# A two-branch spectral filter on one core: strided PSUM writes in the d transform, weights in 128-partition transfers, and a fold moved to VectorE

## The chip, the cores and the metric

The kernel runs on one core of a Trainium2 chip. The metric is the device time of one execution, in microseconds (us), as the median of several runs. Engines are named as in the profile: PE is TensorE's matrix multiply, PEld its weight load, DVE is VectorE, ACT is ScalarE, POOL is GpSimd, SP is SyncE, which here only issues transfers. An "eviction" is the copy of a PSUM tile to SBUF as bf16 by ACT or DVE.

## What is computed

Two filters A and B work on the same input `x` (2048 rows, 1024 columns, bf16). Each takes the real two-dimensional Fourier transform of `x`, multiplies it with its own complex weights (2048 x 513) and transforms back. A gate per row mixes the two.

```
x = A_x
g = _sigmoid((x * gate_w).sum(-1, keepdims=True))
X = rfft2(x)                                   # the same for both filters
a = irfft2(X * (A_w_r + 1j * A_w_i)).astype(bfloat16)
b = irfft2(X * (B_w_r + 1j * B_w_i)).astype(bfloat16)
return g * a + (1 - g) * b
```

## The kernel before, in words

The 2048 rows are 128 x 16, and the transform along the rows is split accordingly, so the whole work is a chain of matmuls with constant matrices. Its stages, with the names that the code gives them:

- **x fold** (`fS`, `fT`, lines 593 to 602). For each of eight pairs of row groups, DVE adds and subtracts the halves of the columns (two instructions of 128x1024).
- **S1** (line 604, 16 of them). Eight matmuls of 256 columns each: the second fold of the columns is done by accumulation, with F and its negative side by side as the moving operand. The eviction is called `Z`. All sixteen `Z` must be there before the next stage starts.
- **Gate** (`gate_row`, `zg`), small matmuls on `Z`.
- **D** (line 637, 16 of them, kg = 0 to 15): the transform along the columns (d), eight matmuls of 256 columns into one PSUM tile of 1024 columns. Four groups of 256 columns stand side by side, and the eviction `Q` (line 651) interleaves two and two of them, so it writes SBUF with a stride of two elements.
- **S2** (line 654, 16 of them): the second part of the row transform, on `Q`; eviction `X`. X is now the spectrum.
- **Products** (`prod`, line 676; eight for each filter, called PA and PB here): DVE multiplies two kg's of X with the weights, two `mul` of 128x2048 and two `sum` of 128x1024.
- **I1** (line 692, 16 for each filter), first part of the inverse; eviction `V`. The column 512 goes a way of its own in small pieces (`x512`, `p512`, `v512`: p5, v5, v5t), and a small transfer (`vrow`) puts it into `V`.
- **Dinv** (line 752, 16 for each filter); eviction `VA` for filter A and `VB` for B.
- **S1i** (line 809, 16): mixes A and B through gate matrices (`gmix` makes them: sig, RA, RB) and does the last row transform; eviction `o`. DVE then unfolds the columns (`h0`, `h1`, `y0`, `y1`), and a transfer takes each pair of row groups out.

The weights are loaded in three chunks of kg (4, 4 and 8; `KC`, line 16), each chunk in two halves of 64 partitions (`pm`), real and imaginary apart (`wpart`, line 515): fourteen transfers a filter, as the first chunk's second half takes two. In the first half of the partitions a chunk is one contiguous run for each partition, in the second half the rows run backwards, each row of 513 elements (1026 bytes) by itself. B's weights go into the memory that held F, so they wait until S1 is over.

**What sets the order.** A planner (`Plan.run`, line 287) is part of the kernel's program. It gives each operation an assumed cost and a rank (`ORDER`, line 18: a start and a step for each kind of work), plays the engines through, and each engine's instructions are emitted in the order that comes out; an eviction goes to ACT or DVE, whichever is free first in that play. On the chip each engine then works its list strictly in that order, with semaphore waits where data comes from another engine. [...] Lines 454, 457, 479, 480 and 485 are the helpers that record all matmuls, all DVE arithmetic, ACT's evictions, DVE's evictions and all transfers, so the profile's groups are told apart by tiles: `PS<-DM,R` is D, `PS<-RING,SK` S2, `PS<-SK,RING` I1, `PS<-DI,R` Dinv, `PS<-R,RING` S1, `PS<-R,FM` and `PS<-RING,DM` S1i, `PS<-RM,ZG` gmix.

Of the kernel before, what the change touches and what calls it, by code (L numbers as in the profile page):

```python
# [9 lines left out]
ALU = mybir.AluOpType  # L10
# [2 lines left out]

NS = 513
NW = 16 * NS
KC = ((0, 4), (4, 8), (8, 16))
CELL = 512
ORDER = {"in": (0, 0), "x": (48.5, 5.31), "gate": (128.3, 6.12), "D": (35.3, 4.27), "S2": (2.5, 7.29),
         "PA": (46.6, 2.74), "IA": (49.9, 4.36), "x5": (67.7, 12), "row": (123.1, 12), "EA": (124.8, 11.5),
         "PB": (99.2, 5.5), "IB": (130, 4.9), "gm": (54.4, 5.49), "EB": (126.2, 10.71), "S": (130, 12),  # L20
         "U": (0.5, 2.73)}
DEPTH = ((0, 2), (2, 4), (4, 8), (8, 12), (12, 16))


# [6 lines left out]
def make_consts():  # L31
# [45 lines left out]
    for z in range(2):  # L77
        for pm in range(2):
            for k2 in range(16):
                for j in range(4):  # L80
                    po = pm * 64 + k2 * 4 + j
                    i, cj, spec = (3 - j if pm else j), pm == 1, False
                    if z == 1:
                        i, cj = ((0, 1, 0, 1), (2, 3, 3, 2))[pm][j], 32 * j + 16 * pm > 64
                        spec = i == 0
                    for q2 in range(16):
                        w = np.exp(-1j * pi2 * q2 * (k2 + cj) / 16)
                        if spec and j == 2:
# [24 lines left out]
        S2[z, 2] = -S2[z, 1]  # L113
# [144 lines left out]
class Plan:  # L258
# [28 lines left out]
    def run(self, keys):  # L287
# [8 lines left out]
        for n in nodes:  # L296
            for p in n.pre:
                p.suc.append(n)
            for t in n.tiles:
                t.left += 1  # L300
        free = {e: 0.0 for e in Sched.ENG}
        cells = {a: [True] * c for a, c in self.arena.items()}
        used = {}
        ready = {e: [] for e in Sched.ENG}
# [42 lines left out]
        for n in nodes:  # L347
            if not n.wait:
                push(n)
        now, count, done = 0.0, 0, 0  # L350
        while done < len(nodes):
            for e in ("sp", "pool", "pe", "act", "dve"):
                if free[e] > now + 1e-9:
                    continue
                for item in ready[e]:
                    n = item[2]
                    if not take(n):
                        continue
                    occ, lat = n.engs[e]
                    n.eng, n.start = e, now  # L360
                    free[e] = now + occ
                    n.end = now + lat
                    if n.dma:
                        dma_free = max(dma_free, now + 1.3) + lat
                        n.end = dma_free + 0.9
                    order.append(n)
                    count += 1
                    heappush(events, (n.end, count, n))
                    heappush(events, (free[e], -count, None))
                    for e2 in n.engs:  # L370
                        ready[e2].remove(item)
                    break
# [32 lines left out]
def bass_gated_mix__spectral_gfnet__spectral_gfnet__prompt_kernel(  # L405
# [11 lines left out]
    def ap(t, off, dims, p0=0, np_=128):  # L417
# [23 lines left out]
    GW = R4  # L441

    P = Plan({"ps": 8, "ring": NCELL, "late": 32},
             {"ps": ("ps", 4), "p1": ("ps", 8), "st": ("ring", 4), "q": ("ring", 3), "t": ("ring", 2),
              "pp": ("ring", 2), "g": ("ring", 1), "vb": ("ring", 4), "o": ("late", 3), "h": ("late", 2),
              "y": ("late", 3), "w": ("ring", 1)})
    xv = A_x[0].rearrange("(p r) d -> p r d", r=16)
# [43 lines left out]
    def rg(t, off, dims, p0=0, np_=128):  # L491
        return ap(R4 if P.limit[t.pool][0] == "late" else RING, t.at * CELL + off, dims, p0, np_)

    def cload(eng, t, off, key, a, b, keys, **kw):
        dma("c_" + key, eng, lambda: [(ap(t, off, [[1, b - a]]).bitcast(dt.uint16), cst[key].ap()[:, a:b])],
            (b - a) * 256e-6, 400, [], keys, **kw)
# [15 lines left out]
    cload("sp", DM, 0, "DM", 0, 2048, ["DM"])  # L512
    cload("sp", SK, 0, "SK", 0, 1792, ["SK"])

    def wpart(b, ci, pm, c):
        P.key = ("in", 1)
        T = WR[b]
        pt = pit[id(T)]
        k0, k1 = KC[ci]
        src = wsrc[b][c]  # L520
        n = src.shape[-1]
        prs = []

        def part(ka, kb, r0, step):
            o = [[n, kb - ka], [1, n]] if step < 0 else [[1, (kb - ka) * n]]
            i = [[step * n, kb - ka], [1, n]] if step < 0 else [[1, (kb - ka) * n]]
            prs.append((AP(T, 64 * pm * pt + c * NW + ka * NS, [[pt, 64]] + o),
                        AP(src.tensor, src.offset + r0 * n, [[32 * n, 64]] + i)))
        if pm == 0:
            part(k0, k1, k0, 1)  # L530
        else:
            if k0 == 0:
                part(0, 1, 16, 1)
            part(max(k0, 1), k1, 32 - max(k0, 1), -1)
        dma("W%d%d" % (b, ci), "sp", lambda: prs, (k1 - k0) * 0.0657, 205, [], [("W", b, ci, pm, c)],
            after=["F", "FN", "FN1"] if b else [], n=len(prs))

    def wkeys(b, cs=(0, 1, 2)):
        return [("W", b, ci, pm, c) for ci in cs for pm in range(2) for c in range(2)]

    for ci in range(3):
        for pm in range(2):
            for c in range(2):
                wpart(0, ci, pm, c)
    cload("sp", DI, 0, "DI", 0, 2048, ["DI"])
    cload("sp", RM, 0, "RM", 0, 2048, ["RM"])

# [45 lines left out]
    def xrows(n2):  # L593
# [4 lines left out]
        xs = [("x", n2), ("x", n2 + 1)]  # L598
        P.add("fS", vt(1024), lambda e: [tt(rg(st, 0, [[1024, 2], [256, 2], [1, 256]]), lo, hi, ALU.add)], xs, [(st, 0, 1), (st, 2, 3)], alloc=[st])
        P.add("fT", vt(1024), lambda e: [tt(rg(st, 512, [[1024, 2], [256, 2], [1, 256]]), lo, hi, ALU.subtract)], xs, [(st, 1, 2), (st, 3, 4)])  # L600
        for r in range(2):
            stage_s1(n2 + r, st, r)

    def stage_s1(m, st, r):
        P.key = ("x", m)
        t = Tile("p1", 2)

        def fns():
            f = []
            for s in range(2):  # L610
                for h in range(2):
                    o = psl(t, (s * 2 + h) * 256, [[128, 2], [1, 128]])
# [4 lines left out]
        pe("S1", [256] * 8, fns, [(st, 2 * r, 2 * r + 1), (st, 2 * r + 1, 2 * r + 2), "F", "FN" if m < 2 else "FN1"], [(t,)], alloc=[t])  # L617
# [10 lines left out]
    for ci in range(3):  # L628
        for pm in range(2):
            for c in range(2):  # L630
                wpart(1, ci, pm, c)

    allz = [("Z", m) for m in range(16)]
    Q, X = {}, {}
# [2 lines left out]
    def stage_d(kg):  # L637
# [3 lines left out]

        def fns():
            f = []
            for g, o in ((0, 0), (3, 256), (2, 512), (1, 768)):
                for h in range(2):
                    qq = (g in (1, 2)) * 4 + h * 2 + (g & 1)
                    f.append(mm(psl(t, o, [[1, 256]]), ap(R3, qq * 2048 + kg * 128, [[1, 128]]),
                                ap(DM, (2 * g + h) * 256, [[1, 256]]), h == 0, h == 1))
            return f
        pe("D", [256] * 8, fns, allz + ["DM"], [(t,)], alloc=[t])  # L650
        ev("Q", 1024, lambda: (rg(q, 0, [[512, 2], [1, 2], [2, 256]]), psl(t, 0, [[512, 2], [256, 2], [1, 256]])),
           [(t,)], [(q, 0, 2)], slow=True, alloc=[q])

    def stage_s2(kg):
        P.key = ("S2", kg)
# [20 lines left out]
    def prod(b, m):  # L676
# [2 lines left out]
        x = ap(R4, 2 * m * 1024, [[1024, 2], [512, 2], [1, 512]])  # L679
        w = ap(T, 2 * m * NS, [[NS, 2], [NW, 2], [1, 512]])  # L680
        ws = ap(T, 2 * m * NS + NW, [[NS, 2], [-NW, 2], [1, 512]])
        r = [("X", 2 * m), ("X", 2 * m + 1)] + wkeys(b, [0 if m < 2 else 1 if m < 4 else 2])
        p = PT[b, m] = Tile("pp", 4)
        for c, (a, op) in enumerate(((w, ALU.subtract), (ws, ALU.add))):
            t = Tile("t", 4)
# [197 lines left out]
```

## Time and profile before

| | us |
|---|---|
| three runs | 138.89, 141.08, 140.5 (median 140.5) |
| the profiled execution, whole | 138.86 |
| its span, first to last instruction | 137.1 |
| ACT busy | 112.7 in 123 instructions |
| transfers | 19.53 MB |

The difference between the profiled execution and its span, 1.8 us, lies around the instructions. The profiled execution is near the lowest of the three runs. "Busy" of PE counts a matmul from start to modelled end; matmuls overlap, so what a matmul costs in a stream is the distance between two starts, and that is worked out from rows that merge a stream of them.

### The profile page before, as it was taken

To read this page: it belongs to the slowest core of one execution; us is meant where nothing else is said; L and a number is where in the kernel's file an instruction comes from. 1 tells how busy PE (TensorE), PEld (TensorE's weight loads), DVE (VectorE), ACT (ScalarE), POOL (GpSimd) and SP (SyncE) were. 2 spreads that over 40 slices of the span, in tenths; PEclk is the share of its full clock that TensorE was granted. 3 is DMA by queue.
4 is the path that set the end of the run, shared out by engine and by line. 5 is a ranking of instruction groups with operands and counts; after the bars stand their busy time and mean duration, and the time that the engine had idled before them with its cause. 6 is when DMAs were issued, how large, how long until landed. Compare 5 with 4: busy or idle time off the path is not lost.

```text
span 137.1 us, 2504 instructions
## 1 busy us (share of the span) xinstructions
PE 124.1 (91%) x1034; PEld 91.2 (67%) x1034; DVE 118.8 (87%) x159; ACT 112.7 (82%) x123; POOL 0.2 (0%) x4
## 2 busy tenths in 40 slices
PE   6859999999999949999977999999999999999930
PEld 2348886767778627766745888778887757666500
DVE  0399977389999679999999999999996889998992
ACT  6458886879989976999888799999787689898960
POOL 0000000000000000000000000000000000000000
PEclk9999999999999999999999999999999999999997
DMA  4999999999999999992000000000000021465254
GB/s 128 412 428 426 367 197 196 205 213 169 168 341 201 199 194 225 177 164 42 0 0 0 6 0 0 0 5 0 0 1 5 0 108 45 170 244 203 82 226 153
DMA packets 8269, 19.53 MB, mean 143 GB/s; under 512 B 961, under 2 KB 5057, under 8 KB 7618
## 3 DMA queue, kind: packets, MB, share of 16 engines
q1 hardware_dynamic: 8112, 19.36, 54.4%
q8 instruction: 8, 0.13, 0.5%
q10 hardware_dynamic: 146, 0.02, 0.1%
q14 instruction: 3, 0.02, 0.1%
HBM read 15.17 MB, written 4.19 MB: 141 GB/s over the span
## 4 chain that ended last, share of the span: by engine, by line
PE 53%; DMA 16%; DVE 15%; ACT 7%; SPq 3%; issue 3%; DVEq 0%
PE PS L454 53%; DMA R<-in_B_w_i_dram 13%; DVE RING L457 10%; ACT R L479 6%; DMA R<-in_A_x_dram 4%; SPq L485 3%; DVE R L480 3%; DVE R L457 1%; ACT RING L479 1%; DVE RING L480 1%; DVE P L457 0%; ACT V L479 0%; DVEq L215 0%; DVE X L480 0%
## 5 line engine op out<-in xcount | busy, mean ns | idle before, releaser
L479 ACT ACTIVATE R<-PS 128x1024 bf16<-128x1024 f32 x77 | 74.6, 1062 | 10.8 <-PE PS L454 10.6
L457 DVE TENSOR_TENSOR RING<-R 128x2048 bf16<-128x2048 bf16 (+1 forms) x48 | 48.3, 1046 | 6.8 <-DMA R<-in_A_x_dram 4.7
L479 ACT ACTIVATE RING<-PS 128x1024 bf16<-128x1024 f32 x28 | 32.4, 1180 | 4.0 <-PE PS L454 3.7
L454 PE MATMUL PS<-SK,RING 128*128 128x256 bf16 x256 | 31.0, 273 | 2.5 <-DVE R L480 1.9
L454 PE MATMUL PS<-DI,R 128*128 128x256 bf16 x256 | 30.5, 273 | 0.0
L454 PEld LDWEIGHTS PS<-SK,RING 128*128 128x128 bf16 x256 | 23.7, 98 | 7.5 <-DVE R L480 2.2
L454 PEld LDWEIGHTS PS<-DI,R 128*128 128x128 bf16 x256 | 24.7, 98 | 5.3 <-ACT R L479 0.2
L480 DVE CAST R<-PS 128x1024 bf16<-128x1024 f32 x19 | 23.2, 1223 | 4.4 <-PE PS L454 4.3
L457 DVE TENSOR_TENSOR R<-R 128x1024 bf16<-128x1024 bf16 (+1 forms) x36 | 21.3, 629 | 0.5
L457 DVE TENSOR_TENSOR RING<-RING 128x1024 bf16<-128x1024 bf16 x32 | 21.0, 689 | 0.1
L454 PE MATMUL PS<-RING,SK 128*128 128x511 bf16 (+1 forms) x96 | 16.9, 308 | 0.1
L454 PE MATMUL PS<-R,RING 128*128 128x256 bf16 x128 | 14.5, 273 | 2.0 <-DVE RING L457 1.4
L454 PE MATMUL PS<-DM,R 128*128 128x256 bf16 x128 | 16.1, 272 | 0.0
L454 PEld LDWEIGHTS PS<-R,RING 128*128 128x128 bf16 x128 | 12.3, 98 | 4.6 <-DVE RING L457 1.7
L454 PEld LDWEIGHTS PS<-DM,R 128*128 128x128 bf16 x128 | 11.6, 97 | 2.8 <-DVE R L480 0.4
L454 PEld LDWEIGHTS PS<-RING,SK 128*128 128x128 bf16 x96 | 7.7, 97 | 6.8 <-DVE RING L480 0.3
L454 PE MATMUL PS<-R,FM 128*128 128x512 bf16 x32 | 9.5, 379 | 0.4 <-ACT R L479 0.4
L454 PE MATMUL PS<-RING,DM 128*128 128x512 bf16 x32 | 9.5, 379 | 0.0
L480 DVE CAST RING<-PS 128x1024 bf16<-128x1024 f32 x4 | 5.1, 1264 | 3.0 <-PE PS L454 3.0
L454 PEld LDWEIGHTS PS<-RING,DM 128*128 128x128 bf16 x32 | 3.1, 98 | 3.8
L454 PE MATMUL PS<-RING 128*128 128x512 bf16 x10 | 4.4, 631 | 1.2 <-DVE RING L555 1.2
L454 PEld LDWEIGHTS PS<-R,FM 128*128 128x128 bf16 x32 | 3.0, 98 | 2.3 <-ACT R L479 0.9
(33 smaller groups left out, 27.3 us busy)
## 6 DMA issues: line engine op xcount, KB each, us to landing
out_dram<-R SPq DMA_DIRECT2D x7, 512.0 KB, 2.6
R<-in_A_x_dram SPq DMA_DIRECT2D x3, 1024.0 KB, 9.5
R<-in_A_w_r_dram SPq DMA_DIRECT2D x2, 513.0 KB, 19.0
R<-in_A_w_i_dram SPq DMA_DIRECT2D x2, 513.0 KB, 20.8
R<-in_B_w_r_dram SPq DMA_DIRECT2D x2, 513.0 KB, 18.5
R<-in_B_w_i_dram SPq DMA_DIRECT2D x2, 513.0 KB, 20.2
R<-in_A_x_dram SPq DMA_DIRECT2D x2, 512.0 KB, 4.6
R<-in_A_w_r_dram SPq DMA_DIRECT2D x3, 256.5 KB, 15.9
```

What stands on the lines that cost most here:

```text
L454: return lambda e: e.matmul(o, l, r, start=start, stop=stop, skip_group_check=True)
L457: return lambda e: e.tensor_tensor(out=o, in0=a, in1=b, op=op)
L479: return [lambda e: e.activation(o, i, ACT.Copy)]
L480: return [lambda e: e.tensor_copy(o, i)]
L485: lambda e: [lambda q, d=d, s=s: q.dma_start(d, s) for d, s in pairs()],
```

## The change

Four things are changed, and the planner's ranks with them.

1. **D writes PSUM with a stride of two columns.** Two groups of 256 columns are written into the even and odd columns of one 512-column half, so the PSUM tile already has the order that S2 reads. The eviction `Q` becomes a plain copy of 1024 contiguous elements, and the planner no longer counts it as slow.
2. **Weights in 128-partition transfers.** The place of a row in the partitions changes from `pm * 64 + ...` to `2 * (...) + pm` in the constants, so that one kg of one part (real or imaginary) is one transfer over 128 partitions, each partition one row of 1026 bytes: 32 transfers a filter instead of 14. A product waits for the four transfers of its own two kg's, no longer for a chunk.
3. **The last pair's second fold on VectorE.** For the pair of row groups 14 and 15 (`FULL`), DVE does the second fold too (`u0`, `u1`, two instructions of 128x1024), and the two S1 of that pair become eight matmuls of 128 columns each, without accumulation.
4. **A new order.** New ranks in `ORDER`; the planner starts each engine's play at 0.8 to 1.0 instead of 0. The order of PE stays near to the one before; the share of evictions between ACT and DVE shifts.

```
-ORDER = {"in": (0, 0), "x": (48.5, 5.31), "gate": (128.3, 6.12), "D": (35.3, 4.27), "S2": (2.5, 7.29),
-         "PA": (46.6, 2.74), "IA": (49.9, 4.36), "x5": (67.7, 12), "row": (123.1, 12), "EA": (124.8, 11.5),
-         "PB": (99.2, 5.5), "IB": (130, 4.9), "gm": (54.4, 5.49), "EB": (126.2, 10.71), "S": (130, 12),
-         "U": (0.5, 2.73)}
+ORDER = {"in": (0, 0), "x": (78.5, 2.44), "gate": (130, 8.58), "D": (48.2, 3.52), "S2": (38, 2.18),
+         "PA": (74, 0.52), "IA": (58.6, 3.71), "x5": (63.6, 12), "row": (130, 5.98), "EA": (113.2, 12),
+         "PB": (105.1, 3.43), "IB": (129.9, 3.29), "gm": (96.8, 2.63), "EB": (40, 12), "S": (80.6, 8.68),
+         "U": (15.2, 7.24)}
+FULL = (14,)
...
-                    po = pm * 64 + k2 * 4 + j
+                    po = 2 * (k2 * 4 + j) + pm
...
-        free = {e: 0.0 for e in Sched.ENG}
+        free = {"pe": 0.8, "act": 1.0, "dve": 0.8, "pool": 0.8, "sp": 0.9}
...
-    def wpart(b, ci, pm, c):
...
+    def wpart(b, kg, c):
         P.key = ("in", 1)
+        T, src = WR[b], wsrc[b][c]
+        pt, n = pit[id(T)], src.shape[-1]
+        step = 32 - 2 * kg if kg else 16
+        dma("W%d" % b, "sp", lambda: [(AP(T, c * NW + kg * NS, [[pt, 128], [1, n]]),
+                                       AP(src.tensor, src.offset + kg * n, [[32 * n, 64], [step * n, 2], [1, n]]))],
+            0.1313, 300, [], [("W", b, kg, c)], after=["F", "FN", "FN1"] if b else [])
...
+        if n2 not in FULL:
+            for r in range(2):
+                stage_s1(n2 + r, st, r)
+            return
+        u = Tile("u", 4)
+        a, b = (rg2(st, o, [[1024, 2], [512, 2], [1, 256]]) for o in (0, 256))
+        sk, uk = [(st, i, i + 1) for i in range(4)], [(u, 0, 4)]
+        P.add("u0", vt(1024), lambda e: [tt(rg(u, 0, [[1024, 2], [512, 2], [1, 256]]), a(), b(), ALU.add)], sk, [(u, 0, 2)])
+        P.add("u1", vt(1024), lambda e: [tt(rg(u, 256, [[1024, 2], [512, 2], [1, 256]]), a(), b(), ALU.subtract)], sk, [(u, 2, 4)])
         for r in range(2):
-            stage_s1(n2 + r, st, r)
+            stage_s1(n2 + r, u, r, True)
...
+            if full:
+                return [mm(psl(t, ((s * 2 + h) * 2 + i) * 128, [[1, 128]]), rg(st, r * 1024 + s * 512 + i * 256 + h * 128, [[1, 128]]),
+                           ap(R2, m * 128, [[1, 128]]), True, True) for s in range(2) for h in range(2) for i in range(2)]
...
-            for g, o in ((0, 0), (3, 256), (2, 512), (1, 768)):
+            for g, o in ((0, 0), (3, 1), (2, 512), (1, 513)):
...
-                    f.append(mm(psl(t, o, [[1, 256]]), ap(R3, qq * 2048 + kg * 128, [[1, 128]]),
+                    f.append(mm(psl(t, o, [[2, 256]]), ap(R3, qq * 2048 + kg * 128, [[1, 128]]),
                                 ap(DM, (2 * g + h) * 256, [[1, 256]]), h == 0, h == 1))
...
-        ev("Q", 1024, lambda: (rg(q, 0, [[512, 2], [1, 2], [2, 256]]), psl(t, 0, [[512, 2], [256, 2], [1, 256]])),
-           [(t,)], [(q, 0, 2)], slow=True, alloc=[q])
+        ev("Q", 1024, lambda: (rg(q, 0, [[1, 1024]]), psl(t, 0, [[1, 1024]])), [(t,)], [(q, 0, 2)], alloc=[q])
...
-        r = [("X", 2 * m), ("X", 2 * m + 1)] + wkeys(b, [0 if m < 2 else 1 if m < 4 else 2])
+        r = [("X", 2 * m), ("X", 2 * m + 1)] + wkeys(b, (2 * m, 2 * m + 1))
```

More of the change, by code (lines that the diff above doesn't have):

```diff
@@ L15 @@
 NW = 16 * NS
-KC = ((0, 4), (4, 8), (8, 16))
 CELL = 512
-ORDER = {"in": (0, 0), "x": (48.5, 5.31), "gate": (128.3, 6.12), "D": (35.3, 4.27), "S2": (2.5, 7.29),
-         "PA": (46.6, 2.74), "IA": (49.9, 4.36), "x5": (67.7, 12), "row": (123.1, 12), "EA": (124.8, 11.5),
-         "PB": (99.2, 5.5), "IB": (130, 4.9), "gm": (54.4, 5.49), "EB": (126.2, 10.71), "S": (130, 12),
-         "U": (0.5, 2.73)}
+ORDER = {"in": (0, 0), "x": (78.5, 2.44), "gate": (130, 8.58), "D": (48.2, 3.52), "S2": (38, 2.18),
[3 more added lines that the diff above has]
+FULL = (14,)
 DEPTH = ((0, 2), (2, 4), (4, 8), (8, 12), (12, 16))
@@ L349, in run @@
                 push(n)
+        for i, (e, t) in enumerate(free.items()):
+            heappush(events, (t, -1 - i, None))
         now, count, done = 0.0, 0, 0
@@ L368, in run @@
                     heappush(events, (n.end, count, n))
-                    heappush(events, (free[e], -count, None))
+                    heappush(events, (free[e], -9 - count, None))
                     for e2 in n.engs:
@@ L443, in bass_gated_mix__spectral_gfnet__spectral_gfnet__prompt_kernel @@
     P = Plan({"ps": 8, "ring": NCELL, "late": 32},
-             {"ps": ("ps", 4), "p1": ("ps", 8), "st": ("ring", 4), "q": ("ring", 3), "t": ("ring", 2),
+             {"ps": ("ps", 4), "p1": ("ps", 8), "st": ("ring", 4), "u": ("ring", 2), "q": ("ring", 3), "t": ("ring", 2),
               "pp": ("ring", 2), "g": ("ring", 1), "vb": ("ring", 4), "o": ("late", 3), "h": ("late", 2),
@@ L492, in rg, with rg2 @@
         return ap(R4 if P.limit[t.pool][0] == "late" else RING, t.at * CELL + off, dims, p0, np_)
+    def rg2(t, off, dims):
+        return lambda: rg(t, off, dims)
     def cload(eng, t, off, key, a, b, keys, **kw):
@@ L513, in bass_gated_mix__spectral_gfnet__spectral_gfnet__prompt_kernel, with wkeys @@
     cload("sp", SK, 0, "SK", 0, 1792, ["SK"])
-    def wpart(b, ci, pm, c):
+    def wpart(b, kg, c):
         P.key = ("in", 1)
[L517 to L544, printed above, removed]
+        T, src = WR[b], wsrc[b][c]
[4 more added lines that the diff above has]
+            0.1313, 300, [], [("W", b, kg, c)], after=["F", "FN", "FN1"] if b else [])
+    def wkeys(b, kgs=range(16)):
+        return [("W", b, kg, c) for kg in kgs for c in range(2)]
+    for kg in range(16):
+        for c in range(2):
+            wpart(0, kg, c)
     cload("sp", DI, 0, "DI", 0, 2048, ["DI"])
@@ L600, in xrows, with stage_s1 @@
         P.add("fT", vt(1024), lambda e: [tt(rg(st, 512, [[1024, 2], [256, 2], [1, 256]]), lo, hi, ALU.subtract)], xs, [(st, 1, 2), (st, 3, 4)])
+        if n2 not in FULL:
[7 more added lines that the diff above has]
+        P.add("u1", vt(1024), lambda e: [tt(rg(u, 256, [[1024, 2], [512, 2], [1, 256]]), a(), b(), ALU.subtract)], sk, [(u, 2, 4)])
         for r in range(2):
-            stage_s1(n2 + r, st, r)
-    def stage_s1(m, st, r):
+            stage_s1(n2 + r, u, r, True)
+    def stage_s1(m, st, r, full=False):
         P.key = ("x", m)
@@ L616, in fns @@
             return f
-        pe("S1", [256] * 8, fns, [(st, 2 * r, 2 * r + 1), (st, 2 * r + 1, 2 * r + 2), "F", "FN" if m < 2 else "FN1"], [(t,)], alloc=[t])
+        if full:
+            pe("S1", [128] * 8, fns, [(st, 0, 2), (st, 2, 4), "F"], [(t,)])
+        else:
+            pe("S1", [256] * 8, fns, [(st, 2 * r, 2 * r + 1), (st, 2 * r + 1, 2 * r + 2), "F", "FN" if m < 2 else "FN1"], [(t,)])
         ev("Z", 1024, lambda: (ap(R3, m * 8, [[128, 128], [1, 8]]), psl(t, 0, [[8, 128], [1, 8]])), [(t,)], [("Z", m)])
@@ L626, in bass_gated_mix__spectral_gfnet__spectral_gfnet__prompt_kernel @@
           [(gzps,), "MS"], ["ZG"])
[L628 to L631, printed above, removed]
+    for kg in range(16):
+        for c in range(2):
+            wpart(1, kg, c)
     allz = [("Z", m) for m in range(16)]
```

## The prediction

> **What bounds the kernel.** First the page's shares and the chain that ended last, then the waits, then the timeline around the longest wait.
>
> ```profile
> PE 124.1 (91%) x1034; PEld 91.2 (67%) x1034; DVE 118.8 (87%) x159; ACT 112.7 (82%) x123; POOL 0.2 (0%) x4
> ...
> PE 53%; DMA 16%; DVE 15%; ACT 7%; SPq 3%; issue 3%; DVEq 0%
> ```
>
> PE is the busiest engine and half the chain. Its real price shows where a stream is merged:
>
> ```profile
> 94.97 1.06 PE L454 MATMUL PS<-RM,ZG 128*128 128x128 bf16 x16
> ...
> 97.67 7.15 PE L454 MATMUL PS<-DI,R 128*128 128x256 bf16 x64
> ```
>
> 64 matmuls of 256 columns take 7.15 us, the last one 0.27 to drain: 0.109 each, 0.87 for a tile of eight. Those of 128 columns cost (1.06 - 0.22) / 15 = 0.056. A tile of S2 or S1i costs 0.9 (S2 alternates with D in 1.79). So PE has 103 us of work between D's start at 23.71 and its end at 131.3; the rest is waits (view of the waits, 48 to 76 us):
>
> ```profile
> DVE RING L457 <- DMA R<-in_B_w_i_dram: 2.0, 1, 2.0
> PE PS L454 <- DVE R L480: 1.9, 1, 1.9
> ...
> PE PS L454 <- ACT V L479: 1.1, 2, 1.0
> ...
> PE PS L454 <- DVE RING L457: 0.6, 1, 0.6
> ```
>
> The timeline says what the first two are:
>
> ```profile
> 45.46 1.29 DVE L457 TENSOR_TENSOR RING<-RING 128x1024 bf16<-128x1024 bf16 x2
> 48.74 1.23 DVE L457 TENSOR_TENSOR RING<-R 128x2048 bf16<-128x2048 bf16 x1 [1.98 <-DMA R<-in_B_w_i_dram]
> 49.88 1.22 DVE L480 CAST R<-PS 128x1024 bf16<-128x1024 f32 x1
> ...
> 51.16 1.05 PE L454 MATMUL PS<-SK,RING 128*128 128x256 bf16 x8 [1.89 <-DVE R L480]
> ```
>
> DVE stands at B's first product until B's first weights land; behind it waits an eviction, and PE waits for that. PE also waits 0.4 on ACT at 130 us. DVE is second: from its first product (30.49) to its last (95.2) it is full: 16 products at 3.48 (rows 2.36 and 1.29, overlapping), 55.7; five evictions spaced 1.14, 5.7; small pieces 1.3; the weight wait 2.0; together 64.7.
>
> **Part 1, D's strided write.** 128 matmuls change. No row shows a long matmul with a stride in its output. Nearest on PE: I1's weights are read with a stride of two and their LDWEIGHTS takes 98 ns, as D's contiguous ones take 97; S2's 511-column matmul writes from an odd column and takes 378 ns against 380. Farther: ACT writes SBUF with a stride of two in 1.32 instead of 1.02, 29% more. Upper end: 256 columns spread over 512 cost like the 512-column rows (two in 0.43, 0.215 each), 0.107 more each, 13.7 in all. Lower end: 0, for a gain has nothing to come from, since the columns streamed stay 256. I take 0, the PE rows being nearest.
>
> The plain `Q` takes 1.02 on ACT (before 1.33, view by form, 24 to 48 us):
>
> ```profile
> L479 ACT ACTIVATE RING<-PS 128x1024 bf16<-128x1024 f32 x9 | 11.8, 1333 | 1.8 <-PE PS L454 1.8
> L479 ACT ACTIVATE R<-PS 128x1024 bf16<-128x1024 f32 x11 | 10.7, 1049 | 0.4 <-PE PS L454 0.4
> ```
>
> I cost that at 0: PE runs without a wait from 23.7 to 48.2, so ACT's 4 us lie beside it. Without that cover it would be worth two weight-load waits of 0.3 on evicted Q's, 0.6 at most.
>
> **Part 2, the weights.** The trace's packet records give the cause of the late landing: a 4104-byte packet took 160 ns while 128-partition transfers ran beside it, and 316 once only 64-partition ones did. The 1026-byte packets took 102 (median), the fastest 45 to 50. Now 4096 packets a filter on 16 engines: at 51 each (half of 102, as the long ones doubled) 13.1 us; bounds 11.5 (45) and 26.1 (102). SK lands at 17.4, so A lands by 30.5, DI and RM by 33.8, B by 47 instead of 64.6. SP: a weight issue took 0.56 to 0.65 and 0.04 to the next, so 64 need 43 us from 4.7; B's first four go out at about 28 to 31 and land near 33, long before DVE wants them at 46.8. SP's B issues wait for S1 (over by 21.5). Behind them on SP are vrow (wanted near 72) and the outputs, clear of it; POOL issues nothing. More waits stand before DVE's products (four transfers each, not four a chunk): the product at 39.72 had four and started on time, so 0; at most 20 x 0.05 (DVEq's step after the B wait) = 1.0.
>
> So PE's 1.9 goes. What is late next? After: D starts at 22.95 (part 3). DVE's new list puts Q1, Q3, Q4 ahead of the first product: D's fifth tile is done 6.2 later, plus the eviction: 30.4, no earlier than before. Up to PB7 it then holds 16 products (55.7), four evictions (4.6) and small pieces (1.1): the end is 91.8 instead of 95.2. PE reaches the tile that needs it at 95.91 - 0.8 - 3.6 (waits) + 1.0 (below) + 0.87 (one Dinv more ahead) = 93.4, so PE stays the bound. In between, PB1 is done at 30.4 + 9 x 3.48 + 4.6 + 1.1 + 3.48 = 70.9, where PE is at about 70.5; and A's third, sixth and eighth product come within 0.5 of PE's need. I put 1.0 for these four. The 0.6 and the 1.1 of before go, since PA7 (67.3) and the small pieces no longer stand behind the 2.0; ACT's 0.4 goes because the last Dinv of A is moved ahead.
>
> **Part 3, the second fold.** Sixteen S1 matmuls go from 0.109 to 0.056: -0.85. DVE's `u0`, `u1` cost 2 x 0.61 (spacing of the folds): its last fold ends at 18.4, so they end at 19.7, before S1 of row group 14 starts at 20.5: hidden. Z12 behind them is wanted at 19.8. The last Z ends near 22.7 and the three gate tiles (about 1.4) at 22.9: D starts at 22.95, -0.8.
>
> [...]
>
> **Part 4, the order.** PE's list is almost the old one. The tail shifts: from B's first Dinv on DVE has seven evictions where it had four. 28 unfold steps at 0.61, eight short ones at 0.4, seven evictions at 1.14: 28.3 beside PE's 32 tiles, 27.7. DVE has no slack left there, and its last `y` trails PE's end by about 1.0 more than now: +0.9. Bounds: 0 (ACT's share falls by three) and +3.4 (all three evictions exposed).
>
> **Sum**, against the profiled execution (138.86, span 137.07): -0.8 (S1), -4.0 (waits 1.9, 1.1, 0.6, 0.4), +1.0 (new near ties), +0.9 (tail) = -2.9, so 136.0. The median stands 1.64 above that execution. Some of that spread may be the weights' landing, which now is hidden, so I put 0.6 of it on top: 136.6. Alone, this case runs from 134.2 (no near ties, no tail) to 139.0 (tail and DVE's waits exposed).
>
> **Rivals.**
>
> *D's write is slow, and the kernel is slower.* If each written column costs PSUM as much as the pair of columns it lies in, D costs 0.215 a matmul. All 16 D tiles lie before the last S2 on PE, which has no slack there, so +13.7; the near tie at A's sixth product and part of PB1's go, -0.6: 149.7. It decides from 0.025 more a matmul on (3.2 us undo the gain). For it: nothing in the trace excludes it, since no such write is there. Against it: strided reads and odd-start writes on PE cost nothing. With ACT's 29% it would be 0.031 x 128 = 4.0: 140.6, no change.
> [...]
>
> *The weights come no faster.* At 102 ns B's last transfer lands at 17.4 + 2 x 26.1 + 3.3 = 73, B's first four at 50. DVE's `p512` of filter B waits for all of B and now stands near 63, ahead of PA7: DVE loses 2.7 + 6, PE about 7: 143.6. It decides from about 85 ns a packet. Against it: the halving of the 4104-byte packets.
>
> *The waits only move.* DVE is as full as PE: if the near ties cost 1.0 each and the tail its 3.4, -2.9 becomes +2.6: 142 at most, likelier 139.5.
>
> **Chances.** Forecast 0.58; D at twice the price 0.24; D at a part of it 0.08; weights no faster 0.04; waits only move 0.06. The range leaves out the worst of the slow D and the best of the forecast: 134.0 to 150.0; the forecast's own is 134.2 to 139.0. A difference under 2% (137.7 to 143.3 around 140.5) can't be told from no change here. Faster: 0.44, three quarters of the forecast. Within: 0.29, its last quarter, the partly slow D and most of the moved waits. Slower: 0.27, D at twice the price and most of the weights' rival.
>
> **What would show it.** D's group at 272 ns a matmul and its stream at 0.109 says part 1 is free; a step near 0.215 there is the rival. No wait of DVE on in_B_w; B landing near 47. S1 ending 0.8 earlier. PE's waits between 48 and 76 near 1 us. DVE without gaps after 105 us. Wrong would be: a longer D stream, DVE standing at `p512`, or PE waiting for DVE beyond 2 us.

## The result and the profile after

The changed kernel takes 151.28 us (median of four runs, 150.11 to 151.53), the kernel before in the same comparison 139.69 (138.47 to 141.08): ratio 1.0845, 95% interval 1.0719 to 1.0971. It is slower, and its time is close to the 149.7 of the first rival, which had D's write at twice the price. The profiled execution took 151.53, its span is 149.74 (before 138.86 and 137.07).

The page of after, busy shares and the chain that ended last:

```profile
PE 136.2 (91%) x1034; PEld 96.6 (64%) x1034; DVE 119.1 (80%) x160; ACT 110.1 (74%) x124; POOL 0.2 (0%) x4
...
PE 66%; DVE 17%; DMA 7%; issue 5%; ACT 1%; SPq 1%; DVEq 1%
```

PE's share stayed at 91% of a longer span: it has 12 us more work in as many instructions. DVE and ACT have about as much work as before, in a span 12.7 longer. Groups by form, after (mean ns of one behind the busy time, then the idle time before them and what ended it):

```profile
L456 PE MATMUL PS<-DM,R 128*128 128x256 bf16 x128 | 29.6, 417 | 0.0
...
L481 ACT ACTIVATE RING<-PS 128x1024 bf16<-128x1024 f32 x25 | 25.6, 1028 | 13.7 <-PE PS L456 13.7
...
L482 DVE CAST RING<-PS 128x1024 bf16<-128x1024 f32 x7 | 8.6, 1225 | 12.5 <-PE PS L456 12.5
```

D's matmul takes 417 ns where it took 272, as the same group of the kernel before shows:

```profile
L454 PE MATMUL PS<-DM,R 128*128 128x256 bf16 x128 | 16.1, 272 | 0.0
```

The plain eviction `Q` is as short as hoped (1.03 in ACT's row, which holds other evictions too; its twelve `Q` alone take 1.02), and ACT and DVE spend the gain, and more, waiting for PE. PE's timeline where D begins, in after and then before:

```profile
22.64 5.36 PE L456 MATMUL PS<-DM,R 128*128 128x256 bf16 x24
27.79 1.10 PE L456 MATMUL PS<-RING,SK 128*128 128x512 bf16 x6
28.75 1.89 PE L456 MATMUL PS<-DM,R 128*128 128x256 bf16 x8
```

```profile
23.71 2.79 PE L454 MATMUL PS<-DM,R 128*128 128x256 bf16 x24
```

Twenty-four D matmuls in 5.36, the last one 0.417 long: (5.36 - 0.417) / 23 = 0.215 from start to start, where it was (2.79 - 0.272) / 23 = 0.109. A tile of D takes 1.72 instead of 0.87, a tile of S2 beside it 0.96 instead of 0.92.

### The profile page after: what moved, and what is told of

Same layout as the page of the kernel before. It is cut to its first block, busy times and chain, and to the rows that moved or that the text cites. A ratio compares the mean times of both kernels' runs of the same rounds, so it can differ in the third digit from the quotient of the medians.

```text
span 149.7 us, 2569 instructions
## 1 busy us (share of the span) xinstructions
PE 136.2 (91%) x1034; PEld 96.6 (64%) x1034; DVE 119.1 (80%) x160; ACT 110.1 (74%) x124; POOL 0.2 (0%) x4
## 4 chain that ended last, share of the span: by engine, by line
PE 66%; DVE 17%; DMA 7%; issue 5%; ACT 1%; SPq 1%; DVEq 1%
PE PS L456 66%; DVE R L459 9%; DVE RING L459 6%; DMA R<-in_A_x_dram 3%; DMA out_dram<-R 3%; ACT R L481 1%; DVE R L482 1%; DVE RING L482 1%; SPq L487 1%; DVEq L215 1%; DVE P L459 1%
## 5 line engine op out<-in xcount | busy, mean ns | idle before, releaser
L481 ACT ACTIVATE R<-PS 128x1024 bf16<-128x1024 f32 x81 | 78.9, 1053 | 15.7 <-PE PS L456 15.7
L481 ACT ACTIVATE RING<-PS 128x1024 bf16<-128x1024 f32 x25 | 25.6, 1028 | 13.7 <-PE PS L456 13.7
L456 PE MATMUL PS<-DM,R 128*128 128x256 bf16 x128 | 29.6, 417 | 0.0
L459 DVE TENSOR_TENSOR RING<-RING 128x1024 bf16<-128x1024 bf16 x34 | 22.0, 687 | 0.9 <-PE PS L456 0.8
L482 DVE CAST R<-PS 128x1024 bf16<-128x1024 f32 x15 | 18.3, 1223 | 5.2 <-PE PS L456 4.9
L456 PEld LDWEIGHTS PS<-DM,R 128*128 128x128 bf16 x128 | 16.2, 131 | 9.3 <-ACT R L481 0.4
L482 DVE CAST RING<-PS 128x1024 bf16<-128x1024 f32 x7 | 8.6, 1225 | 12.5 <-PE PS L456 12.5
L456 PE MATMUL PS<-R,RING 128*128 128x256 bf16 (+1 forms) x128 | 13.6, 266 | 2.0 <-DVE RING L459 1.4
L456 PEld LDWEIGHTS PS<-RING,SK 128*128 128x128 bf16 x96 | 9.0, 105 | 7.2
L541 ACT ACTIVATE R<-R 128x256 bf16<-128x256 bf16 (+1 forms) x2 | 2.0, 1048 | 3.3 <-DMA R<-c_F 3.3
```

What stands on the lines that cost most here:

```text
L456: return lambda e: e.matmul(o, l, r, start=start, stop=stop, skip_group_check=True)
L459: return lambda e: e.tensor_tensor(out=o, in0=a, in1=b, op=op)
L481: return [lambda e: e.activation(o, i, ACT.Copy)]
L482: return [lambda e: e.tensor_copy(o, i)]
L541: lambda e, a=a, b=b: [lambda e: e.activation(ap(R2, 2048 + a, [[1, b - a]]), ap(R2, a, [[1, b - a]]), ACT.Copy, scale=-1.0)],
```

## The experiments

In the order in which they are told. e1, e3, e4, e5, e7 and e10 to e14 start from the changed kernel, e2, e6, e8 and e9 from the kernel before. "D to last y" runs from D's first matmul to the end of DVE's last unfold, "tail" from the start of PE's last matmul to that end; all are read off the timelines of the profiled executions, one for each kernel.

| kernel | ratio to before (95%) | span | S1 start to D | D to last y | tail |
|---|---|---|---|---|---|
| before | | 137.07 | 17.47 | 110.87 | 3.49 |
| after | 1.0845 (1.0719 to 1.0971) | 149.74 | 16.64 | 124.59 | 4.67 |
| e1 | 0.9927 (0.9879 to 0.9975) | 136.9 | 16.64 | 111.26 | 4.91 |
| e2 | 1.0763 (1.0667 to 1.0859) | 148.8 | 17.97 | 121.82 | 3.49 |
| e5 | 0.9857 (0.9772 to 0.9942) | 135.4 | 16.62 | 109.64 | 4.41 |
| e6 | 0.9850 (0.9817 to 0.9883) | 135.0 | 17.51 | 108.79 | 3.49 |
| e7 | 0.9776 (0.9734 to 0.9818) | 134.5 | 16.62 | 109.10 | 5.01 |
| e8 | 1.0005 (0.9964 to 1.0045) | 137.3 | 17.43 | 111.10 | 3.48 |
| e9 | 0.9686 (0.9562 to 0.9810) | 134.4 | 16.61 | 108.71 | 3.48 |
| e10 | 0.9660 (0.9571 to 0.9749) | 134.7 | 17.08 | 108.50 | 3.84 |
| e12 | 0.9705 (0.9624 to 0.9787) | 133.4 | 16.62 | 108.08 | 3.99 |

By the intervals, after and e2 are more than 2% slower than the kernel before, and e12 is more than 2% faster. So is e10, but the runs of the kernel before beside e9 and e10 scatter most (139.61 to 141.67), so these two ratios are the least sure. e1, e6 and e8 lie within 2% of the kernel before; whether e5, e7 and e9 do can't be told.

**e1: part 1 undone, e2: part 1 alone.** The edit of e1, and of e2 the other way round in the kernel before:

```
-            for g, o in ((0, 0), (3, 1), (2, 512), (1, 513)):
+            for g, o in ((0, 0), (3, 256), (2, 512), (1, 768)):
-                    f.append(mm(psl(t, o, [[2, 256]]), ...
+                    f.append(mm(psl(t, o, [[1, 256]]), ...
-        ev("Q", 1024, lambda: (rg(q, 0, [[1, 1024]]), psl(t, 0, [[1, 1024]])), ...
+        ev("Q", 1024, lambda: (rg(q, 0, [[512, 2], [1, 2], [2, 256]]), psl(t, 0, [[512, 2], [256, 2], [1, 256]])), ...
```

> The changed kernel with part 1 undone: D writes contiguous columns and the eviction Q interleaves them again; weights, fold and the order of every engine stay as in the changed kernel. Theory (D's strided write is the whole loss): D's stream falls from 0.215 to 0.109 a matmul, 13.6 us of PE work go, and the time is 136 to 138.5, that is the prediction's sum for the other three parts. Rival (the rest of the change loses as well, by its order or its 64 transfers): D's stream is as short, but the time stays above 140.

> The kernel before with part 1 alone: D writes with a stride of two, Q is a plain copy, the order of every engine is unchanged. Theory: D's stream is 0.215 a matmul, +13.7 us of PE work; the wait for B's weights (1.9 on PE) goes, because PE comes there later, and perhaps 1 more of the waits at 71 to 75 us, so the time is 149.5 to 152.5. Rival (the slow D needs something else of the change, such as the transfers beside it or the new order): D's stream is shorter than 0.15 and the time under 146.

e1 took 138.50 us, the upper end of what was expected, e2 150.44, within it. Groups by form of e1 (ACT's row from D's stage, 22 to 75 us, alone), then of e2:

```profile
L456 PE MATMUL PS<-DM,R 128*128 128x256 bf16 x128 | 15.9, 272 | 0.0
...
L481 ACT ACTIVATE RING<-PS 128x1024 bf16<-128x1024 f32 x12 | 15.7, 1342 | 0.7 <-PE PS L456 0.7
```

```profile
L454 PE MATMUL PS<-DM,R 128*128 128x256 bf16 x128 | 29.7, 417 | 0.0
```

The slow matmul goes with part 1 in both kernels, and part 1 alone gives most of the loss. In e2 the D stage is 13.6 dearer in matmuls, but D to last y grew by 10.95 only: B's weights, late in the kernel before, are now there when DVE comes, so its 2.0 and PE's 1.9 behind it went, and some small waits too: in the kernel before, the steps of D's matmuls add up to 16.40, 2.45 more than 128 x 0.109.

**e3 and e4: what the price goes by.** e3 writes the columns in pairs, `[[4, 128], [1, 2]]`, which spread over the same 512 columns; e4 writes 128 columns a matmul with a stride of four, in twice as many matmuls:

```
-                    f.append(mm(psl(t, o, [[2, 256]]), ap(R3, ...), ap(DM, (2 * g + h) * 256, [[1, 256]]), h == 0, h == 1))
+                    for i in range(2):
+                        f.append(mm(psl(t, o + 2 * i, [[4, 128]]), ap(R3, ...), ap(DM, (2 * g + h) * 256 + 128 * i, [[1, 128]]), ...
```

> The changed kernel, but D's columns go out in pairs: two neighbouring columns, then two left free for the other group, so 256 columns still spread over 512, while every aligned pair of fp32 columns is full. The order of the columns within each four is then not the one that the next stage expects; that is left as it is, only the time counts. Theory (the price is per pair of columns touched): D's stream is back at 0.109 a matmul and the time at that of the run with contiguous columns, 136 to 138.5. Rival (the price is per span of PSUM, or for any pattern that is not contiguous): D's stream stays at 0.215 and the time near 151.

> The changed kernel, with each D matmul of 256 columns split into two of 128 that write with a stride of four columns (the same 512 columns of PSUM are filled, in an order that the next stage does not expect; only the time counts). Twice as many D matmuls, the same number of columns. Theory (every written column costs the time of a pair, however far apart the columns are): 0.107 for a matmul of 128 columns, so D and the time stay as with stride two, near 151. Rival (the price grows with the span that a matmul covers): 0.215 for each of the 256 matmuls, D's work doubles again by 27 us, near 178. Second rival (a matmul of 128 columns costs 0.056 there too): D is short and the time near 138.

One run each: 137.25 and 151.43 us. Groups of e3, then of e4:

```profile
L456 PE MATMUL PS<-DM,R 128*128 128x256 bf16 x128 | 15.9, 272 | 0.0
```

```profile
L456 PE MATMUL PS<-DM,R 128*128 128x128 bf16 x256 | 29.9, 312 | 0.0
```

The span of columns that is written costs nothing (e3: 512 columns, 272 ns). A stride of four costs what a stride of two costs: 29.9 us of busy PE for 256 columns times 128, against 29.6. So the price goes by the written columns that lack their neighbour, and not by whether the pattern is contiguous: e3's isn't, and it has 15.9 us of busy PE, as contiguous columns have in e1. That each column has its neighbour isn't enough, though, as e11, below, shows.

**e11, e13 and e14: is it the neighbour, or the aligned pair?** All three split each D matmul into 254 and 2 columns: in e11 pairs that start on odd columns, in e13 pairs on even ones, in e14 single columns. The edit of e11:

```
+            for g, o in ((0, 1), (3, 3), (2, 513), (1, 515)):
...
+                    rest = [[509, 2]] if o % 512 == 1 else [[1, 2]]
+                    for p, d, c, n in ((o, [[4, 127], [1, 2]], 0, 254), (o // 512 * 512 + (0 if o % 512 == 1 else 510), rest, 254, 2)):
+                        f.append(mm(psl(t, p, d), ap(R3, ...), ap(DM, (2 * g + h) * 256 + c, [[1, n]]), h == 0, h == 1))
```

> The changed kernel with each D matmul split in two: 254 columns written as pairs of neighbours four apart that start on an odd column (1 2, 5 6, ... for one group, 3 4, 7 8, ... for the other), and the last 2 columns by themselves; the order of the columns in the spectrum differs, so another computation of the same size. The pairs that started on even columns cost nothing (272 ns in the group, a step of 0.109); a step of two or four single columns cost a step of 0.215 and 417 ns. Theory (what costs is each aligned pair of PSUM columns touched, so a pair across the border counts twice): about 415 ns in the group of 254 columns and a D tile near 1.7 to 1.9. Rival (any two neighbouring columns go together): near 270 ns, and a D tile of 0.87 plus what the eight small matmuls add, 0.2 to 0.45. The total is not asked.

> The control to the odd pairs: the same split of each D matmul into 254 and 2 columns, the 254 as pairs four apart that start on an even column; the column order differs again, so another computation of the same size. Odd pairs took 375 ns for the 254, a step of 0.170, then 0.070 for the 2, so 0.240 for the two together and 1.92 a tile. Theory (each aligned pair of PSUM columns touched is the price, so even pairs are free): about 0.109 and 0.03 to 0.06, together 0.14 to 0.17, a tile of 1.1 to 1.35, and 272 ns in the group. Rival (what made the odd pairs dear is the split into two matmuls): 0.24 together and 1.92 a tile, as with odd pairs.

> The second control: the same split, the 254 columns written as single columns with a stride of two as in the changed kernel; the last 2 the same way, so it computes the whole reference. Theory (a pair across a border costs as much as two single columns): 0.24 for the two matmuls together, 1.92 a tile, as with odd pairs. Rival (a pair across a border is cheaper than two singles): 0.25 to 0.28 together, a tile of 2.0 to 2.2, with the 254 near 417 ns.

Unlike its expectation says, e14 doesn't compute the whole reference; no run shows the reason. Matmuls, columns and writes are as described in all three, and in after a D matmul that starts a sum and one that adds to it have the same step, 0.216. Spans 152.3, 140.0 and 152.4. Groups by form of e11, e13 and e14:

```profile
L456 PE MATMUL PS<-DM,R 128*128 128x254 bf16 x128 | 32.4, 375 | 0.0
...
L456 PE MATMUL PS<-DM,R 128*128 128x2 bf16 x128 | 26.8, 209 | 0.0
```

```profile
L456 PE MATMUL PS<-DM,R 128*128 128x254 bf16 x128 | 19.1, 269 | 0.0
L456 PE MATMUL PS<-DM,R 128*128 128x2 bf16 x128 | 17.9, 168 | 0.0
```

```profile
L456 PE MATMUL PS<-DM,R 128*128 128x254 bf16 x128 | 32.4, 375 | 0.0
...
L456 PE MATMUL PS<-DM,R 128*128 128x2 bf16 x128 | 26.8, 209 | 0.0
```

And the first three tiles of D on PE in e13 and in e14 (a row merges both forms):

```profile
23.02 3.43 PE L456 MATMUL PS<-DM,R 128*128 128x254 bf16 x48
26.31 1.05 PE L456 MATMUL PS<-RING,SK 128*128 128x512 bf16 x6
```

```profile
23.49 5.91 PE L456 MATMUL PS<-DM,R 128*128 128x254 bf16 x48
29.26 1.05 PE L456 MATMUL PS<-RING,SK 128*128 128x512 bf16 x6
```

From the first start to S2's start there are 24 couples: 3.29 / 24 = 0.137 with even pairs, 5.77 / 24 = 0.240 with singles. Odd pairs gave 0.240 too, and the same rows as singles to the nanosecond. (Their 375 ns is less than the 415 that was expected, because a part of the price shows at the small matmul: steps of 0.170 and 0.070, where even pairs have 0.108 and 0.029.) So the split isn't what cost, and two neighbours across an odd border count as two singles: the price goes by each aligned pair of fp32 columns that is touched. Half-used pairs cost 0.240 - 0.137 = 0.103 for 254 columns, about one column's time (0.109 / 256) more for each column.

**e5 and e8: the interleaving without the price.** D writes contiguously, and the eviction reads PSUM by a step of 256 columns and writes plainly; e8 has that in the old order, where D was contiguous already:

```
-        ev("Q", 1024, lambda: (rg(q, 0, [[1, 1024]]), psl(t, 0, [[1, 1024]])), ...
+        ev("Q", 1024, lambda: (rg(q, 0, [[512, 2], [2, 256], [1, 2]]), psl(t, 0, [[512, 2], [1, 256], [256, 2]])), ...
```

> The changed kernel with D contiguous, and the eviction Q doing the interleaving on its reading side: it reads PSUM with a step of 256 columns between neighbours and writes SBUF contiguously. Order unchanged. Theory (only where the write is strided does an eviction pay): Q takes 1.02 on ACT like a plain copy, against 1.32 with the strided write, and the time is that of the run with contiguous columns and the old eviction, within 0.5, as PE hides it. Rival (a jumping read of PSUM costs ACT as much as the strided write): 1.3 or more for Q.

> The kernel before with nothing changed but Q's access patterns: it reads PSUM with the step and writes SBUF contiguously, in the old order of all engines. Theory (a shorter eviction is hidden by PE, as the prediction had it): Q is 0.3 shorter on ACT, the time within 0.4 of before. Rival (the eviction's length reaches PE at the waits for PSUM tiles and Q's, as the difference of 0.8 between the two contiguous versions of the changed kernel suggests): 0.6 to 1.2 less.

e5 took 137.66 us; e8 138.81, ratio 1.0005 (0.9964 to 1.0045). ACT's group in e5 (22 to 75 us, as for e1):

```profile
L481 ACT ACTIVATE RING<-PS 128x1024 bf16<-128x1024 f32 x12 | 12.2, 1042 | 1.0 <-PE PS L456 1.0
```

The read with a step is nearly as short as the plain copy (1.042 against 1.023 in after; the strided write of e1 1.342). In the old order the shorter `Q` is worth nothing (e8). In the new one it is worth 0.8 by the medians and 111.26 - 109.64 = 1.6 in the profiled executions (e1 against e5), more than the 0.5 that the expectation of e5 allowed: there ACT's evictions reach PE. In e1, PE's weight loads wait for them between 22 and 65 us, and e5 has no such row:

```profile
PEld PS L456 <- ACT RING L481: 1.9, 6, 0.4
```

After against e5 has nothing else of weight than D's write: the stage from D to the last S2 takes 52.71 against 39.06, 13.65 more. D to last y takes 14.95 more; where the other 1.3 come from is told below.

**e6: the weights alone, e9: all but D's write and the order.** e6 takes only part 2 into the kernel before. e9 adds part 3 (`FULL = (14,)`) and e5's eviction, all in the old order.

> The kernel before with part 2 alone: 32 transfers of 128 partitions a filter, and the order of every compute engine unchanged. Theory: DVE's wait of 2.0 for B's weights and PE's 1.9 behind it go, but DVE then spends about 1.0 (24 semaphore waits at 0.042, read from the gap of 1.18 for 28 in the changed kernel) ahead of filter B's column 512, so the time falls by 1.0 to 2.0. Rival (the 64 transfers cost elsewhere what they save): within 0.5 of the kernel before.

> The kernel before in its own order, with three changes: weights in 128-partition transfers, the last pair's second fold on VectorE, and ScalarE's and VectorE's evictions of Q reading PSUM by a step of 256 columns with plain writes (D's matmuls write contiguous columns). It computes the whole reference. Theory (the parts' gains are independent of the order, and the new order's longer tail is not taken): the weights alone gave a span of 135.0 (2.0 less), the fold takes 0.8 off the first stage, the old tail of 3.5 from the last matmul to the last store stays: span about 134.2, ratio 0.975 to 0.980. Rival (the fold's 0.8 is lost again in the D stage, since the old order's evictions stand elsewhere): span 135.0, ratio 0.985, as the weights alone. The stage from the first matmul to D's first matmul tells it apart: 16.6 in both cases, with the D stage 0.8 longer in the rival.

136.73 and 136.50 us. PE's waits in e6, 24 to 136 us:

```profile
PE PS L454 <- ACT V L479: 1.1, 2, 1.0
PE PS L454 <- DVE RING L457: 0.6, 1, 0.6
PE PS L454 <- ACT R L479: 0.4, 1, 0.4
```

The wait of 1.9 is gone and D to last y fell by 2.08, just over the 1.0 to 2.0 expected, but the other three waits of before are all still there: they never hung on the weights. The fold took 0.86 off the way to D and nothing grew for it behind, so e9's theory held, at a span of 134.4 (its ratio, 0.969, is lower than the expected 0.975 to 0.980, which lie within its interval). The gap of 1.0 that one theory wanted in e6 wasn't there: DVE's many waits for B's weights run there from 67.6 to 68.7, beside a product of 1.22 that starts at 67.6.

**e7: one engine collects the waits.** To e5 GpSimd adds a memset that waits for B's 32 transfers; `p512` waits for that alone.

```
+    wb = P.add("wb", {"pool": (0.1, 0.2)}, lambda e: [lambda e: e.memset(ap(WD, 0, [[1, 8]]), 0.0)], wkeys(1), ["WB"])
+    wb.eng = "pool"
...
+        n.reads = ["X5", "WB"]
```

> The kernel of the run with contiguous D and Q reading with the step, with one more thing: GpSimd, which is idle, waits for all of B's transfers and sets a few elements, and DVE's column-512 instruction of filter B waits for GpSimd alone instead of for 28 transfers. The order of all engines stays. Theory (DVE's gap of 1.18 there is the 28 semaphore waits, one after the other): the gap goes, PE's waits of 0.7 on DVE P and 0.9 on DVE RING between 60 and 73 us shrink by 1.0 or more in all, and the time falls by 1.0 to 1.5, to about 136.4. Rival (the gap is the landing of the last transfer, or something else that comes due then): GpSimd waits as long, and the gap and the time stay.

135.85 us; D to last y 0.54 less than e5, about half of what was expected. From D's start to PE's last matmul it is 1.14 less (104.09 against 105.23), but the tail is 0.60 longer: DVE waits 1.3 there for an output buffer, 0.7 in e5. What it removes is seen in after, DVE's timeline around `p512` of filter B (the time in brackets is the idle time before):

```profile
76.36 0.17 DVE L459 TENSOR_TENSOR P<-P 128x16 bf16<-128x16 bf16 x1
77.70 0.21 DVE L459 TENSOR_TENSOR P<-X,R 128x32 bf16<-128x32 bf16 x1 [1.18 <-issue]
```

All of B's weights had landed at 54.0, and yet DVE stood 1.18 there: 28 transfers not waited for before, each with a wait of its own that was long met. In the trace they are fourteen wait instructions, most for two transfers, 0.098 from start to start; 1.18 / 28 = 0.042 for each transfer. In e7 that gap isn't there.

**e10 and e12: the tail.** To e7, evictions moved from DVE to ACT: `VB3`, `VB9` and one `o` in e10, only the two `VB` in e12. The edit of e12:

```
+    for n in P.order:
+        if (n.name, n.key[1]) in (("VB", 3), ("VB", 9)):
+            n.eng = "act"
```

> The changed kernel with D contiguous, Q's evictions reading PSUM by a step of 256 columns and GpSimd collecting the waits of B's weights (the run of that kind had a span of 134.5 and 5.0 from the last matmul to the last store), with three late evictions moved from VectorE to ScalarE. It computes the whole reference. Theory (the new order's longer tail comes from what VectorE has to do after the last matmuls): the tail falls from 5.0 to between 3.5 and 4.0, span 133.0 to 133.5, ratio 0.967 to 0.971. Rival (the tail is set by the last stores and ScalarE's own evictions): the tail stays near 5.0 or PE waits for ScalarE instead, span 134.5 or more, ratio 0.977 or more.

> As the run with three late evictions moved to ScalarE, but only the two of VB3 and VB9 moved, the one of o10 left on VectorE. It computes the whole reference. With three moved, the tail from the last matmul to the last store fell from 5.0 to 3.8, but ScalarE then ran from 117.3 to 128.3 without a gap, and PE waited 1.0 for it at 126.8. Theory (each moved eviction takes 1.14 off VectorE's list and puts 0.9 on ScalarE's, and ScalarE had a gap of 0.5 there): the tail is near 4.0 to 4.6, PE's wait for ScalarE at the end under 0.5, span 133.5 to 134.2. Rival (ScalarE has no room for even two): PE waits 0.9 or more and the span is 134.5 or more.

136.24 and 135.21 us. PE at the end of e10, and DVE's last list in e12:

```profile
126.25 0.59 PE L457 MATMUL PS<-RING,DM 128*128 128x512 bf16 x2
127.87 0.38 PE L457 MATMUL PS<-R,FM 128*128 128x512 bf16 x1 [1.02 <-ACT RING L482]
```

```profile
121.06 1.22 DVE L483 CAST R<-PS 128x1024 bf16<-128x1024 f32 x1
122.19 8.67 DVE L460 TENSOR_TENSOR R<-R 128x1024 bf16<-128x1024 bf16 x17
```

With three moved, the tail shrank by 1.2, but PE waited 1.0 for ACT (e7 0.7) and its last matmul started 0.6 later after D: half of the theory, the rest as its rival had it. D to last y fell by 0.6; the span didn't, since D itself began 0.7 later than in e7, ahead of anything that the edit touches. With two, the tail is 3.99, PE's wait 0.6 (under 0.5 was expected), the span 133.4, just under what was expected. So 1.0 of the 1.5 by which e7's tail is longer than before is DVE's extra evictions. e12 has the shortest span and the lowest median; against e9 and e10 it wasn't timed on one chip, and the intervals overlap, so which of the three is fastest stays open.

## Why the prediction was wrong

**Part 1 is the step that failed:** "I take 0, the PE rows being nearest". Measured: 0.106 more for each matmul, 13.65 for the stage, its upper end (13.7). Those rows were near in the engine, not in the resource: the strided weight load (98 ns against 97) reads SBUF, and the 511 columns from an odd column (378 ns against 380) still fill all their pairs but one. No long matmul of the kernel before writes PSUM with half-used pairs, so "nearest" decided nothing. The first rival had place, size and mechanism right ("each written column costs PSUM as much as the pair of columns it lies in"; nothing of before shows that, e4, e11, e13 and e14 do), and D's 16 tiles do all lie ahead of the last S2 on an engine without slack. `Q`'s gain at 0 was right for the old order (e8); in the new order the shorter `Q` is worth 0.8 to 1.6, more than the 0.6 that I allowed without cover, since S2 waits for `Q` there (e1).

The measured median, 151.28, lies above the range too: its upper end, 150.0, had hardly any room above the rival's 149.7. For the profiled execution the rival's sum is 136.0 + 13.7 - 0.6 = 149.1, and that execution took 151.53, 2.4 more. Half of that, 1.2, is in all that isn't D: e5's profiled execution took 137.15 where the forecast had 136.0. The rest is behind D. The 0.6 of near ties that I let go stayed (S1 began 0.6 earlier than in e5, which takes as much off), and PE got a new wait (waits of after, 48 to 90 us):

```profile
PE PS L456 <- ACT R L481: 1.5, 1, 1.5
DVE P L459 <- issue: 1.2, 1, 1.2
PE PS L456 <- DVE RING L459: 0.9, 2, 0.8
...
PE PS L456 <- DVE P L459: 0.7, 1, 0.7
```

A's first Dinv stands 1.5 at 88.7, where the small transfer `vrow` has just landed (88.6); in e5 it stands 0.2. The view names ACT for this wait, but the transfer is what came last. The slow D isn't the reason: `vrow` is issued 62.4 after D's start against 48.9 in e5, which is D's price and no more, and e4, with a D as slow, has the short wait. The transfer itself took longer, 3.5 from issue to landing instead of 1.8. The views of the transfers of after and of e5 give, as the last number, the median of filter A's `vrow` and B's:

```profile
R<-V SPq DMA_DIRECT2D x2, 4.0 KB, 2.6
```

```profile
R<-V SPq DMA_DIRECT2D x2, 4.0 KB, 1.7
```

In the trace's packet records of after, fifteen of its sixteen packets start from 86.33 to 86.48, and the last one only at 87.48, when an instruction load of 16384 bytes that began at 86.24 has ended (1.26 long). e13 has the same picture and a `vrow` of 3.6. So most of the 1.3 by which D to last y grew beyond the D stage's price came from this meeting; that the packet waited for the load is read from these times alone. Whether it happened in the other three runs of after, one of which took 1.4 less (150.11), isn't known.

**Part 2:** right in the mechanism. The 1026-byte packets took 47 ns in the median (predicted 51, before 102). The page of after, the last number being us from issue to landing:

```profile
R<-in_A_w_r_dram SPq DMA_DIRECT2D x16, 128.2 KB, 7.1
...
R<-in_B_w_r_dram SPq DMA_DIRECT2D x16, 128.2 KB, 3.3
```

A's last landed at 31.3 (predicted 30.5). B's last landed at 54.0, not 47: SP issued B's 32 from 30.0 to 51.7, 0.68 each, and my sum left the issues out as a bound on the landing, although by my own count they ended at 4.7 + 43 = 47.7, after the 47. No work waited for that, so nothing in the time hangs on it. DVE doesn't wait on `in_B_w` any more, and the weights alone are worth 2.08 (e6; predicted 1.9). "So 0; at most 20 x 0.05" for the waits was too low at `p512` of filter B: 1.18, of which 0.54 reached the end (e7).

The sum took three more waits of before (1.1, 0.6, 0.4) as gone, and set 1.0 of new ties against them. With the weights alone they stay (e6). In the new order e5 has 0.9 and 0.7 on DVE and 0.4 and 0.2 on ACT instead, 2.2: "the waits only move" was right for these, and the -4.0 and +1.0 should have been about -1.8 (4.0 before, 2.2 in e5).

**Part 3:** right. S1's start to D fell by 0.83 in after and 0.86 in e9 (predicted 0.85 less in S1's matmuls, D 0.8 earlier), and `u1` ended at 19.6 (19.7).

**Part 4:** +0.9 for the tail; measured +1.2 in after and +1.5 in e7, with the reason given (e12: two evictions off DVE, 1.0 back). "DVE gapless after 105" didn't hold in after, since a late PE leaves DVE gaps, and e7 has one of 1.3 for an output buffer. On the whole the order loses 0.9 against the old one (D to last y, e5 109.64, e9 108.71), and 0.5 of that is the gap that e7 takes away.

Without D's write the other parts came to a ratio of 0.986 (e5), where the forecast stood at 136.0 / 138.86 = 0.979; the interval, 0.9772 to 0.9942, includes that.

## What to carry to other kernels

A matmul into PSUM should fill aligned pairs of fp32 columns (0.109 us for 256 columns here, 0.215 where each column is alone in its pair); where two groups have to be interleaved one by one, let the eviction's read do it, which cost 0.02 an eviction on ACT here (1.042 in e5, 1.023 in after), and not PE's write, which cost double. When no row shows an operation, look for rows that load the same memory in the same way; a row of the same engine that loads another said nothing here (the strided weight load's 98 ns against 97), and with a bottleneck engine and a bound of 13.7 against a break-even at 3.2, the unknown decides the sign. Waits that a profile lists side by side are counted as gone only if each hangs on the thing removed.

## What the hardware showed that was not expected

- PSUM writes by aligned pairs: 0.109 us for 256 columns that fill their pairs, and the same 272 ns and 15.9 us of busy PE whether the pairs are neighbours (e1) or not (e3); 0.215 with a stride of two, and as much busy PE with a stride of four (29.6 in after, 29.9 in e4). Pairs across an odd border cost what single columns do: 0.240 for a couple of 254 and 2 columns in e11 and e14, 0.137 with even pairs in e13.
- A part of the write's price shows at the next matmul: a 2-column matmul had a step of 0.029 behind 254 columns in even pairs (e13) and 0.070 behind 254 singles (e14), whose own step was 0.170. In e11 the step is 0.070 also where the 2 columns fill one aligned pair, so it is the matmul ahead that counts.
- A PSUM read with a step of 256 columns costs ACT 0.02 an eviction (1.042 in e5 against 1.023 in after), an SBUF write with a stride of two elements 0.3 (1.33 before). On DVE that write costs 0.1 (1.31 in e1 against 1.22 in e5).
- Semaphore waits that were long met cost 0.042 each on DVE where they stood in a row with only short instructions ahead (28 of them, 1.18, in after), and nothing seen beside a product of 1.22 (e6).
- `vrow` took 3.52 us in after and 3.58 in e13, 1.73 to 1.77 in the other fourteen kernels. In both slow cases one of its 256-byte packets started only when an instruction load of 16384 bytes had ended, 1.26 and 1.40 long.
